# A decode step with cached attention and a gated MLP: two w_out blocks in one six-group transfer, their products dealt round the column groups, and fewer, wider copies

## The chip, the core and the metric

The kernel runs on one core of a Trainium2 chip. The metric is the device time of one execution in microseconds (us); three executions of the kernel before the change gave a median of 709.77 us (709.28 to 710.01). Every number is in fp32.

The engines are named as in the profile: PE multiplies matrices (PEld loads its stationary operand), DVE and POOL work on vectors, ACT does activations, SP issues transfers. The transfers themselves are moved by 16 DMA engines that all of the core's queues share.

## What is computed

One token for each of 8 batch rows, width 512. With `xn = layernorm(x)`:

```python
q = (xn @ wq).reshape(8, 32, 128)                 # wq: 512 x 4096
k, v = repeat(cache, 4)                           # 8 kv heads, 4096 positions, 128 wide
s = softmax(q . k * 128**-0.5) . v                # per batch row and head
s = s.reshape(8, 4096) @ wo                       # wo: 4096 x 512
z = gelu(xn @ w_in)                               # w_in: 512 x 1792
z1, z2 = z[:, :896], layernorm(z[:, 896:])
g = silu((z1 * (w_sp * z2 + b_sp)) @ w_out)       # w_out: 896 x 512
out = x + s * g
```

The keys are loaded in 16 pieces of 8.4 MB, the values in as many; with `wq`, `wo` and the MLP's weights about 291 MB are read.

## The kernel before, in words

All large operands pass through `ring`, a pool of three slots of 128 x 16384 fp32 (8.4 MB each). A slot can be loaded again when the last instruction that reads it is done. SP issues the loads in the order of the program text, and an issue that waits for its slot holds back all issues behind it. The order is: the MLP's weights (slot 1), `wq` (slot 2), keys of head 0, first half of the batch (slot 3, "k00"), keys of head 0, second half ("k01", slot 1 again), values "v00" (slot 2 again), "v01" (slot 3 again), keys of head 1 "k10", and so on for 8 heads, then `wo` in seven pieces.

PE also takes its work in the order of the text: `mlp()`, `project_q(0)`, `project_q(1)`, then for each head `scores` for two halves, `softmax`, `values` for eight batch rows, and last the product with `wo`. So slot 1 is free for k01 when the last product of `mlp()` that reads weights is done, slot 2 is free for v00 when `project_q(1)` is done, and slot 3 for v01 when the first `scores` is.

PE's array is used in four column groups of 32 columns (`R = 32`, `G = 4`): a product with at most 32 output rows is written to partitions 32g to 32g+31 of a PSUM bank, and products for different g can be issued one after another.

`mlp()` computes `xn @ w_in` (L144), gelu, the inner layernorm and the gate on DVE (L148 to L177), and then the product with `w_out`, here called the tail. The 896 rows of `w_out` are seven blocks of 128 rows. Blocks 0, 2, 4 and 6 (`MAIN`) lie on 128 partitions, behind `w_in` in the transfer `w_mlp` (L66). Blocks 1, 3 and 5 lie on few partitions: three transfers `w_low` (L72) of 8, 4 and 2 groups of `LOW_R = 4` rows bring them as 22 chunks of 32, 16 and 8 rows, side by side in the columns. For the tail, the gated activations `u` are transposed on PE (L179 for `MAIN`, L192 for the chunks), copied to SBUF by DVE (L180, L193) and multiplied: four `MAIN` products, one per column group (L184), and 22 chunk products (L196). A chunk of block j goes to column group `j // 2`, so that chunks that follow one another mostly share a group:

```python
for i, (j, r) in enumerate(some):
    g = j // 2
    nc.tensor.matmul(pw[R * g:R * (g + 1), :], hL[p0:p0 + n, i, R * g:R * (g + 1)],
                     w_low[:, lo + i, :], start=False, stop=((j, r) in LAST))
```

PSUM tiles named `scr` come from a pool of two banks used in turn; the tail's sum `pw` lies in `sc`, a fixed bank.

`project_q` writes the queries into `qz` by 32 copies of 128 x 4 for each quad of heads (L226), and `softmax` writes the transposed weights into `pT` by four copies of 128 x 128 per 512 columns (L270). `values` reads `pT` as `pT[:, j, b, :]` (L280).

Outside the tail, the change touches the tile of `xn` (L118), `hy` (L134, L135), `qz` (L86) and the host's packing of `w_out` (L366 to L385).

Of the kernel before, what the change touches and what calls it, by code (L numbers as in the profile page):

```python
# [8 lines left out]
F32 = mybir.dt.float32  # L9
# [4 lines left out]
P = 128  # L14
B, D = 8, 512
HKV, REP, S, DH = 8, 4, 4096, 128
NK = D // P
G = 4
J = S // (G * P)
R = 32  # L20
# [21 lines left out]


@with_exitstack
def tile_gqa_gmlp_decode(ctx: ExitStack, tc: tile.TileContext, x, side, kT, v, wq, wo,
                         w_mlp, lows, out):
# [22 lines left out]
    low_sb = []  # L69
# [10 lines left out]
    ident = const.tile([P, P], F32, name="ident")  # L80
# [20 lines left out]
    sc = ps_fix.tile([P, 2, 512], F32, name="sc")  # L101
# [29 lines left out]
    def mlp():  # L131
        zu = work.tile([P, 4, FQ], F32, name="zu", tag="p")
        z, u = zu[:, :2], zu[:, 2:]
        hy = work.tile([P, 2 * D], F32, name="hy", tag="pT")  # L134
        hT, hL = hy[:, :P], hy[:, P:].rearrange("p (a s) -> p a s", s=P)  # L135
        y_sb, e = zu[:, :2].rearrange("p a f -> p (a f)"), zu[:, 2, :P]
        pz = scratch([P, 2 * FQ], "pz")
        nc.vector.memset(pz, 0.0)
        for part in range(2):
            for k in range(NK):  # L140
                for g in range(G):
                    lo = g * FQ
                    n = min(FQ, FH - lo)
                    nc.tensor.matmul(pz[R * g:R * (g + 1), part * FQ:part * FQ + n], xnT[:, k, :],  # L144
                                     w_in_sb[:, k, part * FH + lo:part * FH + lo + n],
                                     start=(k == 0), stop=(k == NK - 1))
# [30 lines left out]
        nc.vector.tensor_mul(u[:, 1, :], z2, z1)  # L177
        th = scratch([P, P], "th")
        nc.tensor.transpose(th, u[:, 1, :P], ident)  # L179
        nc.vector.tensor_copy(hT, th)  # L180
        pw = sc[:, 0, :]
        for i, j in enumerate(MAIN):
            g = j // 2
            nc.tensor.matmul(pw[R * g:R * (g + 1), :], hT[:, R * g:R * (g + 1)], w_out_sb[:, i, :],  # L184
                             start=True, stop=(j == 6))
        for (ne, p0, _, chunks), w_low in zip(LOW, low_sb):
            n = ne * LOW_R
            for lo in range(0, len(chunks), 4):
                some = chunks[lo:lo + 4]
                tl = scratch([n, len(some) * P], "tl")  # L190
                for i, (j, r) in enumerate(some):
                    nc.tensor.transpose(tl[:, i * P:(i + 1) * P], u[:, 1, P + r:P + r + n], ident)  # L192
                nc.vector.tensor_copy(hL[p0:p0 + n, :len(some)].rearrange("p a s -> p (a s)"), tl)  # L193
                for i, (j, r) in enumerate(some):
                    g = j // 2
                    nc.tensor.matmul(pw[R * g:R * (g + 1), :], hL[p0:p0 + n, i, R * g:R * (g + 1)],  # L196
                                     w_low[:, lo + i, :], start=False, stop=((j, r) in LAST))
        nc.vector.tensor_copy(y_sb, pw)
# [10 lines left out]
    def project_q(quad):  # L209
        pq = scratch([P, REP * DH], "pq")  # L210
        for k in range(NK):
            for g in range(G):
                lo = (quad * G + g) * REP * DH
                nc.tensor.matmul(pq[R * g:R * (g + 1), :], xnT[:, k, :], wq_sb[:, k, lo:lo + REP * DH],  # L214
                                 start=(k == 0), stop=(k == NK - 1))
        q_sb = work.tile([P, REP * DH], F32, name="q_sb", tag="p")
        nc.vector.tensor_scalar(q_sb, pq, float(DH) ** -0.5, None, op0=ALU.mult)
        tq = scratch([P, REP * P], "tq")
        for r in range(REP):
            nc.tensor.transpose(tq[:, r * P:(r + 1) * P], q_sb[:, r * DH:(r + 1) * DH], ident)  # L220
        tv = tq.rearrange("p (r g c) -> p r g c", r=REP, g=G)
        for g in range(G):
            h = quad * G + g
            for b in range(B):
                o = b * R + b * REP
                nc.vector.tensor_copy(qz[:, h, o:o + REP], tv[:, :, g, b])  # L226

# [12 lines left out]
    def softmax(h):  # L240
# [22 lines left out]
        nc.vector.tensor_scalar(p, p, w, None, op0=ALU.mult)  # L263
        pT = work.tile([P, J, B, G * REP], F32, name="pT")
        for c in range(2):
            t = scratch([P, 512], "t")
            for j in range(4):
                nc.tensor.transpose(t[:, j * P:(j + 1) * P], p[:, 4 * c + j, :], ident)  # L268
            for j in range(4):
                nc.vector.tensor_copy(  # L270
                    pT[:, 4 * c + j].rearrange("p b (g r) -> p g b r", g=G),
                    t[:, j * P:(j + 1) * P].rearrange("p (g b r) -> p g b r", g=G, b=B))
        return pT

    def values(b, pT, v_unit):
        o = o_ps[b % 2]
        of = o.rearrange("p g d -> p (g d)")
        for j in range(J):
            c = j % G
            nc.tensor.matmul(of[R * c:R * c + G * REP, :], pT[:, j, b, :],  # L280
                             v_unit[:, j], start=(j < G), stop=(j >= J - G))
        o_all = small.tile([P, G, DH], F32, name="o_all")
        nc.vector.tensor_mul(o_all, o, diag[:, :, None].to_broadcast([P, G, DH]))  # L283
        o_sb = small.tile([P, DH], F32, name="o_sb")
        nc.vector.tensor_reduce(o_sb, o_all.rearrange("p g d -> p d g"), op=ALU.add, axis=AX.X)  # L285
        return o_sb
# [110 lines left out]
```

## Time and profile before

| what | value |
|---|---|
| median of three executions | 709.77 us (709.28 to 710.01) |
| the profiled execution, its own time | 710.74 us |
| its span, first to last instruction | 708.9 us |
| PE busy | 417.8 us, 59% of the span |
| DVE busy | 176.7 us, 25% |
| packets on the main DMA queue q1 | 6550, 290.79 MB |
| bytes over the span | 411 GB/s on average |

A row of the page's second part gives 40 slices of 17.7 us each; a digit is the busy share in tenths, and PEclk is the granted clock of PE in tenths of full speed. In a group of instructions, `x44` is the count, followed by the busy time in us, the mean duration of one in ns, and the idle time of the engine just before them with what ended it. One fp32 matmul of the program text stands as two records in the trace. In the chain of waits, each row is a start, a duration and what the time went to. In a table of stretches, DMA is the mean busy share of the 16 DMA engines; a packet counts in the stretch in which it starts, so short stretches can show more than 1.

### The profile page before, as it was taken

Reading aid. Unit: us, or ns where it says so; the run is one execution under the profiler, and the core shown is the slowest. Engines: PE = TensorE matmul, PEld = TensorE weight load, DVE = VectorE, ACT = ScalarE, POOL = GpSimd, SP = SyncE. Lnnn points to the kernel's source line nnn. Section 1 sums busy time; section 2 is a strip of 40 time slices with the busy share of each in tenths; the row PEclk is TensorE's granted clock in tenths of the full one; section 3 lists DMA queues with packets and bytes.
Section 4 is the critical chain, followed back from the end, with each engine's and each line's share of the span. In section 5 each row is a group of like instructions: output and inputs, shape, how many; then the busy total and the mean of one; then the engine's idle time right before and its main releaser. Section 6 shows DMA issues by size and latency. Waiting matters only on the chain.

```text
span 708.9 us, 5936 instructions
## 1 busy us (share of the span) xinstructions
PE 417.8 (59%) x2667; PEld 124.1 (18%) x2667; DVE 176.7 (25%) x376; ACT 13.5 (2%) x27; POOL 3.7 (1%) x11
## 2 busy tenths in 40 slices
PE   2499875545665556554556557554554475655676
PEld 1221222111211112111211112110111121111222
DVE  2400312340144004230234014210234024400450
ACT  0000000000000000000000000000000000000000
POOL 1000000000000000000000000000000000000000
PEclk9655696777677767776777677787777667776797
DMA  9990599999999999999999999999999999999996
GB/s 386 447 404 26 237 415 463 418 423 459 415 429 453 411 436 451 411 440 445 414 441 437 425 433 441 429 430 437 433 426 437 441 422 430 444 423 429 412 427 255
DMA packets 6735, 291.25 MB, mean 411 GB/s; under 512 B 758, under 2 KB 1014, under 8 KB 1406
## 3 DMA queue, kind: packets, MB, share of 16 engines
q1 hardware_dynamic: 6550, 290.79, 95.2%
q8 instruction: 21, 0.34, 0.2%
q10 hardware_dynamic: 160, 0.08, 0.0%
q14 instruction: 4, 0.03, 0.0%
HBM read 290.80 MB, written 0.07 MB: 410 GB/s over the span
## 4 chain that ended last, share of the span: by engine, by line
DMA 72%; PE 22%; issue 4%; DVE 1%; SPq 0%; POOLq 0%; POOL 0%
DMA slot<-in_kT 34%; DMA slot<-in_v 32%; PE sc L237 7%; PE o_ps L280 6%; DMA slot<-in_wo 6%; PE sc L196 5%; PE scr L214 1%; PE sc L340 1%; PE scr L192 1%; PE po_ps L289 0%; DVE o_sb L285 0%; PE sc L184 0%; DMA x_sb<-in_x 0%; DVE o_all L283 0%; SPq L317 0%
## 5 line engine op out<-in xcount | busy, mean ns | idle before, releaser
L237 PE MATMUL sc<-slot,qz 128*32 128x512 f32 x1024 | 148.8, 746 | 122.6 <-DMA slot<-in_kT 122.6
L280 PE MATMUL o_ps<-slot,pT 128*16 128x512 f32 x1024 | 151.8, 733 | 73.9 <-DMA slot<-in_v 73.9
L283 DVE TENSOR_TENSOR o_all<-o_ps,diag 128x512 f32<-128x512 f32 x64 | 44.2, 691 | 148.9 <-PE o_ps L280 148.8
L242 DVE TENSOR_REDUCE nm<-sc 128x1 f32<-128x1024 f32 x8 | 9.8, 1224 | 268.0 <-PE sc L237 268.0
L237 PEld LDWEIGHTS sc<-slot,qz 128*32 128x32 f32 x1024 | 36.1, 133 | 228.8 <-DMA slot<-in_kT 130.5
L285 DVE TENSOR_REDUCE o_sb<-o_all 128x128 f32<-128x512 f32 x64 | 67.8, 1060 | 2.2
L280 PEld LDWEIGHTS o_ps<-slot,pT 128*16 128x16 f32 x1024 | 29.6, 111 | 153.9 <-issue 103.6
L289 PE MATMUL po_ps<-fold,o_sb 128*128 128x4 f32 x128 | 24.7, 263 | 28.4 <-DVE o_sb L285 28.4
L196 PE MATMUL sc<-slot,hy 16*32 16x512 f32 (+2 forms) x44 | 38.8, 1056 | 0.8 <-DVE hy L193 0.8
L289 PEld LDWEIGHTS po_ps<-fold,o_sb 128*128 128x128 f32 x128 | 19.0, 188 | 73.5 <-DVE o_sb L285 72.3
L268 PE MATMUL scr<-ident,p 128*128 128x128 f32 x64 | 15.0, 412 | 10.7 <-DVE p L263 10.7
L244 ACT ACTIVATE p<-sc,nm 128x1024 f32<-128x1024 f32 x8 | 8.9, 1113 | 566.1 <-DVE nm L242 566.1
L270 DVE COPY pT<-scr 128x128 f32<-128x128 f32 x64 | 13.9, 283 | 9.6 <-PE scr L268 9.6
L268 PEld LDWEIGHTS scr<-ident,p 128*128 128x128 f32 x64 | 12.0, 214 | 11.1 <-issue 11.1
L193 DVE COPY hy<-scr 16x512 f32<-16x512 f32 (+3 forms) x6 | 3.8, 635 | 34.9 <-PE sc L196 25.4
L144 PE MATMUL scr<-slot,xnT 128*32 128x256 f32 (+1 forms) x64 | 6.5, 549 | 9.3 <-DMA slot<-in_w_mlp 9.3
L196 PEld LDWEIGHTS sc<-slot,hy 16*32 16x32 f32 (+2 forms) x44 | 6.6, 163 | 27.7 <-issue 23.9
L247 PE MATMUL scr<-ident,nm 128*1 128x128 f32 x8 | 2.2, 270 | 10.9 <-DVE nm L242 10.9
L214 PE MATMUL scr<-slot,xnT 128*32 128x512 f32 x64 | 8.4, 672 | 0.0
L260 PE MATMUL scr<-wl,same 128*128 128x1 f32 x16 | 3.8, 309 | 6.2 <-DVE wl L258 6.2
L331 PE MATMUL sc<-slot,oT 128*8 128x512 f32 x32 | 6.0, 878 | 1.3 <-DMA slot<-in_wo 1.3
L340 PE MATMUL sc<-slot,oT 128*8 128x128 f32 x128 | 5.3, 334 | 1.4 <-DMA slot<-in_wo 1.4
(86 smaller groups left out, 81.9 us busy)
## 6 DMA issues: line engine op xcount, KB each, us to landing
slot<-in_v SPq DMA_DIRECT2D x4, 2048.0 KB, 39.5
slot<-in_wo SPq DMA_DIRECT2D x3, 2048.0 KB, 34.1
slot<-in_w_mlp SPq DMA_DIRECT2D x1, 4608.0 KB, 13.8
slot<-in_wo SPq DMA_DIRECT2D x1, 1024.0 KB
slot<-in_wo SPq DMA_DIRECT2D x1, 512.0 KB, 33.3
slot<-in_wo SPq DMA_DIRECT2D x2, 256.0 KB, 28.9
slot<-in_w_low SPq DMA_DIRECT2D x1, 384.0 KB
slot<-in_w_low SPq DMA_DIRECT2D x1, 256.0 KB
```

Of the source, the lines that this page charges most:

```text
L196: nc.tensor.matmul(pw[R * g:R * (g + 1), :], hL[p0:p0 + n, i, R * g:R * (g + 1)], w_low[:, lo + i, :], start=False, stop=((j, r) in LAST))
L214: nc.tensor.matmul(pq[R * g:R * (g + 1), :], xnT[:, k, :], wq_sb[:, k, lo:lo + REP * DH], start=(k == 0), stop=(k == NK - 1))
L237: nc.tensor.matmul(sc[R * g:R * (g + 1), c, :], qz[:, h, b * R:(b + 1) * R], k_sb[:, i, c, g, :], start=(b == 0), stop=(b == B - 1))
L242: nc.vector.tensor_reduce(m, sc, op=ALU.max, axis=AX.XY, negate=True)
L244: nc.scalar.activation(p.rearrange("p j s -> p (j s)"), sc.rearrange("p c s -> p (c s)"), AF.Exp, bias=m, accum_out=l[:, h:h + 1])
L268: nc.tensor.transpose(t[:, j * P:(j + 1) * P], p[:, 4 * c + j, :], ident)
L270: nc.vector.tensor_copy(pT[:, 4 * c + j].rearrange("p b (g r) -> p g b r", g=G), t[:, j * P:(j + 1) * P].rearrange("p (g b r) -> p g b r", ...
L280: nc.tensor.matmul(of[R * c:R * c + G * REP, :], pT[:, j, b, :], v_unit[:, j], start=(j < G), stop=(j >= J - G))
L283: nc.vector.tensor_mul(o_all, o, diag[:, :, None].to_broadcast([P, G, DH]))
L285: nc.vector.tensor_reduce(o_sb, o_all.rearrange("p g d -> p d g"), op=ALU.add, axis=AX.X)
L289: nc.tensor.matmul(po[:, b * REP:(b + 1) * REP], o_sb, fold, start=True, stop=True)
L340: nc.tensor.matmul(acc[R * g:R * g + B, :], oT[:, h, r, :], wo_sb[:, m, g * P:(g + 1) * P], start=(m == FOLDED), stop=(m == HKV * REP - 1))
```

## The change

Five blocks of `w_out` (0, 2, 4, 6 and now 5) come with `w_mlp` on 128 partitions. The other two (1 and 3) come by one transfer of 6 groups of 4 rows: 24 partitions that each hold, for each block, 6 chunks of 512 columns (five chunks of 24 rows and one of 8; `CH = 6`). The 17 products of the tail (5 and 12) are issued round the four column groups, whatever their block, into a bank of the pool of two instead of `sc`. For them, 2 transposes and one copy prepare the five large products, and 6 transposes and 6 copies the chunks. `xn` moves into unused columns of slot 1, behind the MLP's weights. `qz` rows are 288 instead of 256 long, so that one copy of 128 x 32 per head can write all eight batch rows; `pT` is laid out by batch row first and written by one copy of 128 x 512 per 512 columns.

```diff
-MAIN = [0, 2, 4, 6]
-LOW_R = 4
-def rows_of(j, lo, hi, n):
-    return [(j, r) for r in range(lo, hi, n)]
-LOW = [(8, 0, 0, rows_of(1, 0, P, 32) + rows_of(5, P // 2, P, 32)),
-       (4, 0, 6 * D, rows_of(3, 0, P, 16)), (2, R, 6 * D, rows_of(5, 0, P // 2, 8))]
-LAST = [(1, 96), (3, 112), (5, 56)]
+LOW_E, LOW_R = 6, 4
+QR = LOW_E * LOW_R
+CH = -(-P // QR)
+MAIN = [0, 2, 4, 6, 5]
+LOW = [1, 3]
+N_LOW = len(LOW) * CH * D
...
+    n_low = n_mlp + N_LOW
     nc.sync.dma_start(mlp_slot[:, :n_mlp], w_mlp)
+    nc.sync.dma_start(mlp_slot[:QR, n_mlp:n_low],
+                      w_low[:, :LOW_R * N_LOW].rearrange("e (i n) -> e i n", n=N_LOW))
-    for (e, p0, c0, chunks), w_low in zip(LOW, lows):
-        t = mlp_slot[p0:p0 + e * LOW_R, n_mlp + c0:n_mlp + c0 + len(chunks) * D]
-        nc.sync.dma_start(t, w_low[:, :LOW_R * len(chunks) * D].rearrange("e (i n) -> e i n", i=LOW_R))
-        low_sb.append(t.rearrange("p (c d) -> p c d", d=D))
+    w_low_sb = mlp_slot[:QR, n_mlp:n_low].rearrange("p (j a d) -> p j a d", a=CH, d=D)
...
-    qz = const.tile([P, HKV, B * R], F32, name="qz")
+    qz = const.tile([P, HKV, B * (R + REP)], F32, name="qz")
...
-    xn = work.tile([B, D], F32, name="xn", tag="pT")
+    xn = from_slot(B, D)
...
-        th = scratch([P, P], "th")
-        nc.tensor.transpose(th, u[:, 1, :P], ident)
-        nc.vector.tensor_copy(hT, th)
-        pw = sc[:, 0, :]
...
+        th = scratch([P, 2 * P], "th")
+        for a in range(2):
+            nc.tensor.transpose(th[:, a * P:(a + 1) * P], u[:, 1, a * P:(a + 1) * P], ident)
+        nc.vector.tensor_copy(hT.rearrange("p a s -> p (a s)"), th)
+        for lo in range(0, CH, 4):
+            n = min(4, CH - lo)
+            tl = scratch([QR, n * P], "tl")
+            for a in range(lo, lo + n):
+                k = min(QR, P - a * QR)
+                nc.tensor.transpose(tl[:k, (a - lo) * P:(a - lo + 1) * P],
+                                    u[:, 1, P + a * QR:P + a * QR + k], ident)
+            for a in range(lo, lo + n):
+                k = min(QR, P - a * QR)
+                nc.vector.tensor_copy(hL[:k, a], tl[:k, (a - lo) * P:(a - lo + 1) * P])
+        pw = scratch([P, D], "pw")
+        todo = [(hT[:, j % 2, R * (j // 2):R * (j // 2 + 1)], w_out_sb[:, i, :]) for i, j in enumerate(MAIN)]
+        for a in range(CH):
+            k = min(QR, P - a * QR)
+            todo += [(hL[:k, a, R * (j // 2):R * (j // 2 + 1)], w_low_sb[:k, i, a, :])
+                     for i, j in enumerate(LOW)]
+        for i, (lhsT, rhs) in enumerate(todo):
+            g = i % G
+            nc.tensor.matmul(pw[R * g:R * (g + 1), :], lhsT, rhs, start=(i < G), stop=(i + G >= len(todo)))
         nc.vector.tensor_copy(y_sb, pw)
...
-            for b in range(B):
-                o = b * R + b * REP
-                nc.vector.tensor_copy(qz[:, h, o:o + REP], tv[:, :, g, b])
+            nc.vector.tensor_copy(qz[:, h].rearrange("p (b s) -> p b s", b=B)[:, :, :REP],
+                                  tv[:, :, g, :B].rearrange("p r b -> p b r"))
...
-        pT = work.tile([P, J, B, G * REP], F32, name="pT")
+        pT = work.tile([P, B, J, G * REP], F32, name="pT")
...
-            for j in range(4):
-                nc.vector.tensor_copy(
-                    pT[:, 4 * c + j].rearrange("p b (g r) -> p g b r", g=G),
-                    t[:, j * P:(j + 1) * P].rearrange("p (g b r) -> p g b r", g=G, b=B))
+            nc.vector.tensor_copy(
+                pT[:, :, 4 * c:4 * c + 4].rearrange("p b j (g r) -> p (j g) b r", g=G),
+                t.rearrange("p (m b r) -> p m b r", b=B, r=REP))
...
-            nc.tensor.matmul(of[R * c:R * c + G * REP, :], pT[:, j, b, :],
+            nc.tensor.matmul(of[R * c:R * c + G * REP, :], pT[:, b, j, :],
                              v_unit[:, j], start=(j < G), stop=(j >= J - G))
```

The source of the low transfer on the host is a tensor of 6 rows, each of 4 x 6144 values with 64 values of padding behind.

More of the change, by code (lines that the diff above doesn't have):

```diff
@@ L30 @@
 FOLDED = 16
-MAIN = [0, 2, 4, 6]
-LOW_R = 4
-def rows_of(j, lo, hi, n):
-    return [(j, r) for r in range(lo, hi, n)]
-LOW = [(8, 0, 0, rows_of(1, 0, P, 32) + rows_of(5, P // 2, P, 32)),
-       (4, 0, 6 * D, rows_of(3, 0, P, 16)), (2, R, 6 * D, rows_of(5, 0, P // 2, 8))]
-LAST = [(1, 96), (3, 112), (5, 56)]
+LOW_E, LOW_R = 6, 4
[4 more added lines that the diff above has]
+N_LOW = len(LOW) * CH * D
 @with_exitstack
 def tile_gqa_gmlp_decode(ctx: ExitStack, tc: tile.TileContext, x, side, kT, v, wq, wo,
-                         w_mlp, lows, out):
+                         w_mlp, w_low, out):
     nc = tc.nc
@@ L134, in mlp @@
         hy = work.tile([P, 2 * D], F32, name="hy", tag="pT")
-        hT, hL = hy[:, :P], hy[:, P:].rearrange("p (a s) -> p a s", s=P)
+        hT = hy[:, :2 * P].rearrange("p (a s) -> p a s", a=2)
+        hL = hy[:QR, 2 * P:2 * P + CH * P].rearrange("p (a s) -> p a s", a=CH)
         y_sb, e = zu[:, :2].rearrange("p a f -> p (a f)"), zu[:, 2, :P]
@@ L177, in mlp @@
         nc.vector.tensor_mul(u[:, 1, :], z2, z1)
-        th = scratch([P, P], "th")
-        nc.tensor.transpose(th, u[:, 1, :P], ident)
-        nc.vector.tensor_copy(hT, th)
-        pw = sc[:, 0, :]
[L182 to L197, printed above, removed]
+        th = scratch([P, 2 * P], "th")
@@ L368 @@
     w2 = c(B_w_out).reshape(NB, P, D)
-    lows = {}
-    for i, (e, _, _, chunks) in enumerate(LOW):
-        n = e * LOW_R
-        t = np.stack([w2[j, r:r + n] for j, r in chunks])
-        t = t.reshape(len(chunks), e, LOW_R, D).transpose(1, 2, 0, 3).reshape(e, -1)
-        lows[f"w_low{i}"] = np.concatenate([t, np.zeros((e, 64), np.float32)], axis=1)
+    low = np.zeros((len(LOW), CH * QR, D), np.float32)
+    low[:, :P] = w2[LOW]
+    low = low.reshape(len(LOW), CH, LOW_E, LOW_R, D).transpose(2, 3, 0, 1, 4).reshape(LOW_E, -1)
+    low = np.concatenate([low, np.zeros((LOW_E, 64), np.float32)], axis=1)
     arrays = {
@@ L384 @@
             w2[MAIN].transpose(1, 0, 2).reshape(P, len(MAIN) * D)], axis=1),
-        **lows,
+        "w_low": low,
     }
@@ L391 @@
     with tile.TileContext(nc) as tc:
-        n = len(args) - len(LOW)
-        tile_gqa_gmlp_decode(tc, *args[:n], args[n:], out)
+        tile_gqa_gmlp_decode(tc, *args, out)
     r = run(nc, [{f"in_{name}": a for name, a in arrays.items()}], core_ids=[0])
```

6 lines of the change are left out of this document (5 added, 1 removed).

## The prediction

> **What bounds the kernel now.** I read the page's slices first, then the chain of waits, then what SP's queue waited for, then single stretches.
>
> ```profile
> DMA  9990599999999999999999999999999999999996
> ...
> q1 hardware_dynamic: 6550, 290.79, 95.2%
> q8 instruction: 21, 0.34, 0.2%
> ...
> DMA 72%; PE 22%; issue 4%; DVE 1%; SPq 0%; POOLq 0%; POOL 0%
> ```
>
> The transfers run at nine tenths or more everywhere but in the fourth and fifth slices (53 to 89 us) and at the end. So the kernel is bound by its bytes, with one hole. While q1's packets run, one DMA engine moves 290.79 MB / (16 x 0.952 x 708.9 us) = 26.93 GB/s, all of them 431. The hole, from the chain of waits, SP's waits and the tables of stretches:
>
> ```profile
> 71.25 7.04 PE sc L196 x8
> ...
> 85.76 3.62 PE scr L214 x32
> 89.37 0.02 issue
> 89.39 31.44 DMA slot<-in_v
> ```
> ```profile
> SPq L293 <- PE sc L196: 57.5, 1, 57.5
> SPq L293 <- DMA slot<-in_w_low: 16.3, 3, 11.9
> ```
> ```profile
> 44.00:84.00 40.00, 38.44 (x88) 7.72 (x86) 5.17 (x9) 0.31 (x1) 0.00 (x0) 0.53 0.37 154
> 84.00:700.00 616.00, 353.50 (x2348) 104.42 (x2344) 158.61 (x331) 11.26 (x24) 0.00 (x0) 0.74 1.00 432
> ```
>
> SP stood 57.5 us in front of k01's issue (L293) until the last chunk product of the tail (L196) ended at 78.29. Between 44 and 84 us the engines were busy 0.37 of the time: 0.63 x 40 = 25.2 us of mean idle time. From 84 to 700 us the share is 1.00. Only this hole can be won; what it is worth depends on which of the 16 engines ends last. Its ends:
>
> ```profile
> 3.91 74.73 SPq L293 DMA_DIRECT2D slot<-in_kT  x2
> ```
> ```profile
> DMA to landing us min/median/max: 55.5/55.5/55.5
> ```
> ```profile
> 50.00:51.00 1.00, 1.00 (x2) 0.17 (x1) 0.00 (x0) 0.00 (x0) 0.00 (x0) 0.50 0.91 393
> 51.00:52.00 1.00, 1.00 (x3) 0.27 (x2) 0.00 (x0) 0.00 (x0) 0.00 (x0) 0.50 0.76 328
> 52.00:53.00 1.00, 1.00 (x3) 0.25 (x2) 0.00 (x0) 0.00 (x0) 0.00 (x0) 0.50 0.31 131
> 78.00:79.00 1.00, 0.28 (x1) 0.00 (x0) 0.68 (x1) 0.00 (x0) 0.00 (x0) 0.50 0.00 0
> 79.00:80.00 1.00, 0.94 (x12) 0.60 (x16) 0.22 (x2) 0.00 (x0) 0.00 (x0) 0.50 2.69 918
> ```
>
> The first row is SP's for k00 and k01, the second k00's landing (L293 up to 60 us): issued at 3.91, landed on its last engine 55.5 later, at 59.4. The share falls below one after 50; a packet of 64 KB takes 65.5 / 26.93 = 2.43 us and counts where it starts, so the earliest engines ran dry at about 52.5. k01's packets start at about 79.3, 1.0 us after PE let go. So the earliest engines idled 26.8 us, the last 19.9.
>
> **The change part by part.** *Transfers.* `w_mlp` grows by 128 x 512 x 4 = 262 KB; the low part shrinks from 786 KB to 24 x 24.6 = 590 KB. Together 66 KB more, 0.15 us. `w_mlp` lands 262 / 431 = 0.61 us later, and with it L144 and the chain behind it:
>
> ```profile
> 14.67 6.46 PE L144 MATMUL scr<-slot,xnT 128*32 128x256 f32 x64 [9.32 <-DMA slot<-in_w_mlp]
> 31.17 0.43 DVE L177 TENSOR_TENSOR zu<-zu 128x256 f32<-128x256 f32 x1
> 31.65 0.47 PE L179 MATMUL scr<-ident,zu 128*128 128x128 f32 x1 [2.38 <-DVE zu L177]
> 31.92 1.06 PE L192 MATMUL scr<-ident,zu 128*32 128x128 f32 x4
> 32.16 0.29 DVE L180 COPY hy<-scr 128x128 f32<-128x128 f32 x1 [0.57 <-PE scr L179]
> 32.91 1.94 PE L184 MATMUL sc<-slot,hy 128*32 128x512 f32 x8
> 34.78 7.03 PE L196 MATMUL sc<-slot,hy 32*32 32x512 f32 x8
> 42.38 0.41 DVE L193 COPY hy<-scr 32x256 f32<-32x256 f32 x1 [8.69 <-PE scr L192]
> ```
>
> *The tail before*, from L177's end to 78.29: 46.7 us, of which the 44 records of L196 are most. They run one behind the other: 7.03 us for 8, 0.85 from one start to the next. L184's 8 records, four products in four column groups, need 1.94 us in all: they run beside one another.
>
> *The tail after* starts at 31.6 + 0.6 = 32.2. Two transposes take 0.5 + 0.2 (a further one of L192's four), the first four chunks' about as long as L192's 1.06: 34.0. The copy of the large pair (0.41) lies beside them. `pw` takes the bank of the first chunks, so the products wait for four copies of 24 x 128, by L180's 0.29 and 0.03 between: 35.3. The other two transposes and copies lie beside the first products. 17 products over four groups are five rounds, by L184 1.94 each: 9.7 us. End at 45.0 instead of 78.29.
>
> *The ring later on*, which the change leaves as it is, from the chain of waits:
>
> ```profile
> 131.55 47.35 DMA slot<-in_kT
> ...
> 597.08 49.19 DMA slot<-in_kT
> 646.27 0.04 issue
> 646.32 9.86 PE sc L237 x64
> ```
>
> From 178.90 (131.55 + 47.35) to 646.27 are 24 slots: 19.5 us each, 8.39 MB at 431 GB/s. An issue that lands 49.2 us later has 29.7 us of earlier traffic (49.19 - 19.47) ahead of it, so compute has that much slack per slot.
>
> *What is late next.* k01's issue then stands ready at 45.0, its packets could start at 46.0, and the earliest engine is dry at 52.5 + 0.6 = 53.1. The hole closes with 7 us to spare; that part of the tail's 33 us buys nothing. v00 waits for `project_q`: 78.29 to 89.37 before, 11.1 us, so 56.1 after; it is needed when k01 has gone by, at 53.1 + 19.5 = 72.6. v01 waits for the first `scores`, with k00 landed at about 57 and the longest run of 64 products in the chain 9.9 us, so 67; needed at 92. Behind k01's issue on SP stand exactly these, in this order, and none is late.
>
> *Which engine ends last.* For the earliest engine four terms count. It idled 26.8 us. `w_mlp` takes 0.61 of them. k01's first packets were slow, which a waiting queue spares: 918 KB, 14 packets, start between 79 and 80, and 2.69 x 16 / 14 is 3.07 us each, 0.64 over 2.43. And PE's instructions come by the same engines, 21 packets (q8) of 16 KB, 0.60 us each; one of them came ahead of the hole and was made good in it:
>
> ```profile
> q8 instruction: 1, 0.02, 0.3%
> ```
>
> (the queues between 40 and 60 us). Now it stays on some engine. 26.8 - 0.61 + 0.64 - 0.60 = 26.2 us won. The six groups carry 4 x 24.6 = 98 KB each, 3.65 us; if the engines that have them are also those that fall behind later, 3.65 of the 26.2 are lost: 22.5. If the engine that ends last is spared `w_mlp`'s part and the instructions, the most is 27.4. I take 26.2, the end nearest to the mean row's 25.2 - 0.15 = 25.0: the groups' 3.65 us need not add up with delays that 21 packets spread over other engines.
>
> A rule of the Trainium skill bears on how the groups fall: "DMA: Bandwidth & Descriptors", section "Why a DMA increments its semaphore by 16 and not by 1", says that such a transfer uses the largest number of engines up to 16 that divides the outer sizes of both sides, which for 6 and 24 is six. No row here numbers the engines; by that rule one engine would not get it all, which is a rival below.
>
> *Copies.* L226's and L270's work lies beside transfers:
>
> ```profile
> L270 DVE COPY pT<-scr 128x128 f32<-128x128 f32 x64 | 13.9, 283 | 9.6 <-PE scr L268 9.6
> L226 DVE COPY qz<-scr 128x4 f32<-128x4 f32 x64 | 4.6, 150 | 1.5 <-PE scr L220 1.5
> L325 DVE COPY oT<-po_ps 128x32 f32<-128x32 f32 x8 | 1.5, 191 | 3.8 <-PE po_ps L289 3.8
> L198 DVE COPY zu<-sc 128x512 f32<-128x512 f32 x1 | 0.7, 691 | 7.1 <-PE sc L196 7.1
> ```
>
> 64 small `qz` copies (4.6 us) become 8 of about 0.19 (L325): 3.1 us less of DVE, twice half of it after a `project_q`, inside v00's and v01's slack. Four `pT` copies (1.13) become one of 0.69 (L198): 0.9 us less per head ahead of `values`, which then wait for the landing of v. Worth nothing, and in the 29.7 us if it goes the other way. `xn` in slot 1 would cost something if it had to wait for the slot's transfers; L144 read the slot at 14.67 while SP still waited for `w_low` (16.3 us from about 4, so until 20), so columns, not slots, are waited for. Even then the tail would end at about 51, still in time. `qz`'s wider clearing makes one POOL instruction an eighth longer, in the 9.32 us in which L144 waits for its data.
>
> *Sum*: 710.74 - 26.2 = 684.5 for an execution like the profiled one, whose span would be 682.7. The median of the runs shown is 0.97 lower: 709.77 - 26.2 = **683.6 us**.
>
> **Rivals.** *The products do not overlap.* All chunks use the same rows of the array, and L196 never shows two groups in turn. Then 34 records at 0.85 and the start at 35.3 give 64.5; k01 starts 78.3 - 64.5 = 13.8 us earlier: 696.0. A rule of the Trainium skill says so: "TensorE: Matmul & The Clock Gate", "Part 3: Packing small matmuls", has a weight load overlap a running product only when the row group differs. L184 speaks against it, four products with the same rows in 1.94 us, so I hold it unlikely.
>
> *The low transfer goes by one engine.* 590 KB at 26.93 GB/s are 21.9 us; k00 lands there at 53.1 + 21.9 = 75.0, and every later slot waits for that engine: 26.2 - 21.9 = 4.3 us won, 705.5. Against it: SP waited for `w_low` only until 20, and k00's engines ended between 52.5 and 59.4, so the old transfers with 8, 4 and 2 groups were shared.
>
> *Slower: the wide `pT` copy.* It writes 128 runs of four elements with larger strides. If a run cost what L226's 4-element copy does, 150 ns, a copy would take 19.2 us and `softmax` 36 us more per head. From 29.7 us per head on the ring runs dry: 6.4 us for each of 8 heads, 51 us, 683.6 + 51 = 735. Against it: L270's copies have 32 such runs already and take 0.283.
>
> *It doesn't do what it says*: something else, not the tail, frees slot 1. Then 709.8. Against it stands SP's row, a single wait of 57.5 us for L196.
>
> **How the numbers follow.** Forecast 0.85; no overlap 0.07; one engine 0.03; slower copy 0.03; no effect 0.02. The measurement tells 0.2%, 1.4 us, from no change. Faster: 0.85 + 0.07 + 0.03 = 0.95; same 0.02; slower 0.03. The range takes the forecast's two ends, 709.77 - 22.5 = 687.3 and 709.77 - 27.4 = 682.4, with half a us for repeats: 681.9 to 687.8. The rivals lie outside it and hold 0.15.
>
> **What would show it.** Right: the slices of DMA without a hole; SP's long wait for the tail's last product down from 57.5 to about 24 us; 34 records of products in about 10 us; k00's last engine done at 57 and k01's at 76; the last `wo` landing about 26 us earlier; landings still 19.5 apart. Wrong: the products' records 0.85 apart in a line (no overlap); a landing of k00 at 75 (one engine); a `pT` copy of several us; DMA below 9 in any slice after the third; or landings more than 19.6 apart, with an engine that carries both a low group and the later delays.

## The result, and the profile after

The kernel after the change takes 685.42 us (median of four executions, 685.31 to 687.15). The kernel before, run beside it, takes 709.52 us (median of four, 709.27 to 710.01). The ratio is 0.9665, with a 95% interval of 0.9648 to 0.9682: 24.1 us less, where 26.2 were forecast. The profiled execution took 685.31 us and has a span of 683.5; before it was 710.74 and 708.9, so the two spans differ by 25.4.

The first view is the page: its DMA slices, the queues and the chain's shares by engine.

```profile
DMA  9999999999999999999999999999999999999995
...
q1 hardware_dynamic: 6510, 290.85, 98.7%
q8 instruction: 20, 0.33, 0.2%
...
DMA 80%; PE 15%; issue 4%; DVE 1%; SPq 0%; POOLq 0%; POOL 0%
```

The hole in the fourth and fifth slices is gone. The bytes are the same within 0.06 MB, the share of q1 rises from 95.2% to 98.7%, and DMA's part of the chain from 72% to 80%. The queue of SP says the same, as its waits for the tail and for the low transfer show:

```profile
SPq L295 <- PE scr L201: 22.3, 1, 22.3
...
SPq L295 <- DMA slot<-in_w_low: 3.5, 1, 3.5
```

SP now stands 22.3 us in front of k01's issue where it stood 57.5. The chain of waits at that place:

```profile
34.87 6.27 PE scr L201 x34
41.15 36.29 DMA slot<-in_kT
```

The tail ends at 41.14 instead of 78.29, and k01 lands 36.3 us after its issue, behind k00. In the table of stretches, the third row is the one that showed 0.37 before; the first two are the tail's products:

```profile
34.80:38.20 3.40, 3.33 (x10) 0.56 (x10) 0.41 (x3) 0.00 (x0) 0.00 (x0) 0.51 0.85 366
38.20:41.20 3.00, 2.90 (x25) 0.66 (x24) 0.04 (x1) 0.00 (x0) 0.00 (x0) 1.00 1.18 508
44.00:84.00 40.00, 23.60 (x172) 6.67 (x168) 3.15 (x12) 0.00 (x0) 0.00 (x0) 0.77 1.00 430
84.00:675.00 591.00, 326.35 (x2208) 97.20 (x2196) 150.01 (x217) 11.27 (x24) 0.00 (x0) 0.75 1.00 431
```

The engines are busy from 44 us to the end at 1.00. No other wait for PE leaves them idle. So the time came from the place that the prediction named; what is left to explain is why 24 to 25 us came and not 26.2, and which part of the change did it.

For both questions the ends of the single DMA engines are needed. Each transfer is counted off by 16 engines; the table has the first and the last of the 16 for k00, for k01 and for the last piece of `wo`, in us from the start of the span, of all the kernels that follow. It is worked out from the landings in each trace.

```
kernel          tail ends  k00 landed     k01 landed      last wo piece    last-first  span   median us
before            78.29    52.61..59.43   99.48..101.33   700.37..705.11      4.7      708.9   709.52
after             41.14    53.26..58.08   72.61..77.44    673.22..679.99      6.8      683.5   685.42
e1_one_group      51.1     53.15..59.08   73.43..78.43    674.06..682.07      8.0      685.6   685.95
e2_two_groups     41.6     53.16..58.73   72.62..78.09    673.12..681.70      8.6      685.2   685.82
e3_old_copies     40.3     53.10..58.19   72.46..77.55    672.98..680.28      7.3      683.8   685.96
e4_low_twice      39.3     53.14..61.68   72.49..81.03    673.25..683.53     10.3      687.2   689.33
e5_before_round   49.0     52.63..59.46   71.99..78.81    672.52..680.43      7.9      684.4   686.03
e6_all_main       38.3     54.53..56.32   73.88..75.67    674.42..679.41      5.0      683.0   684.80
e7_one_low4       40.3     53.75..57.30   73.10..76.65    674.01..678.68      4.7      682.2   684.19
e8_low_first      53.4     53.23..57.73   75.37..77.58    675.93..680.66      4.7      684.2   686.68
e9_one_column     62.3     53.29..58.79   83.63..85.53    684.21..689.14      4.9      692.9   695.04
```

The first engine ends 700.37 - 673.22 = 27.15 us earlier than before, the last 705.11 - 679.99 = 25.1. The profiled executions of e1 and e2 took 688.14 and 687.65 us, 2.2 and 1.8 above their medians, so the last landings in their rows are those of longer executions.

### The profile page after: what moved, and what is told of

Same layout as the page of the kernel before. It is cut to its first block, busy times and chain, and to the rows that moved or that the text cites. A ratio compares the mean times of both kernels' runs of the same rounds, so it can differ in the third digit from the quotient of the medians.

```text
span 683.5 us, 5757 instructions
## 1 busy us (share of the span) xinstructions
PE 373.0 (55%) x2634; PEld 115.1 (17%) x2634; DVE 168.0 (25%) x272; ACT 13.5 (2%) x27; POOL 3.9 (1%) x11
## 3 DMA queue, kind: packets, MB, share of 16 engines
q1 hardware_dynamic: 6510, 290.85, 98.7%
## 4 chain that ended last, share of the span: by engine, by line
DMA 80%; PE 15%; issue 4%; DVE 1%; SPq 0%; POOLq 0%; POOL 0%
DMA slot<-in_kT 41%; DMA slot<-in_v 35%; PE sc L240 8%; PE o_ps L282 5%; DMA slot<-in_wo 4%; PE scr L201 1%; PE po_ps L291 0%; DMA x_sb<-in_x 0%; DVE o_sb L287 0%; PE scr L188 0%; SPq L302 0%; DVE hy L192 0%; DVE o_all L285 0%; DVE st L119 0%; PE scr L181 0%
## 5 line engine op out<-in xcount | busy, mean ns | idle before, releaser
L240 PE MATMUL sc<-slot,qz 128*32 128x512 f32 x1024 | 144.1, 726 | 136.1 <-DMA slot<-in_kT 136.1
L271 PE MATMUL scr<-ident,p 128*128 128x128 f32 x64 | 14.8, 410 | 10.7 <-DVE p L266 10.7
L272 DVE COPY pT<-scr 128x512 f32<-128x512 f32 x16 | 11.1, 692 | 10.8 <-PE scr L271 10.8
L145 PE MATMUL scr<-slot,xnT 128*32 128x256 f32 (+1 forms) x64 | 6.4, 547 | 9.6 <-DMA slot<-in_w_mlp 9.6
L201 PE MATMUL scr<-slot,hy 24*32 24x512 f32 (+2 forms) x34 | 6.2, 726 | 0.5 <-DVE hy L192 0.5
L266 DVE TENSOR_SCALAR p<-p,w 128x1024 f32<-128x1024 f32 x8 | 6.0, 753 | 0.3
L145 PEld LDWEIGHTS scr<-slot,xnT 128*32 128x32 f32 x64 | 3.4, 161 | 12.2 <-issue 12.1
```

What stands on the lines that cost most here:

```text
L201: nc.tensor.matmul(pw[R * g:R * (g + 1), :], lhsT, rhs, start=(i < G), stop=(i + G >= len(todo)))
L240: nc.tensor.matmul(sc[R * g:R * (g + 1), c, :], qz[:, h, b * R:(b + 1) * R], k_sb[:, i, c, g, :], start=(b == 0), stop=(b == B - 1))
L272: nc.vector.tensor_copy(pT[:, :, 4 * c:4 * c + 4].rearrange("p b j (g r) -> p (j g) b r", g=G), t.rearrange("p (m b r) -> p m b r", b=B, r ...
```

## The experiments

My theory after the result had two parts. *The tail:* the products dealt round the column groups run beside one another, so k01's issue is ready before the engines run dry, and everything beyond that is worth nothing. *The engines:* the last engine ends later against the first one (6.8 us, before 4.7) because one of the six that carry a low group also carries instruction packets. The rivals: the order round the groups does not matter, since the repacking alone shortens the tail enough; or the copies brought a part of it; or the last engine's lag has nothing to do with the low groups.

**e1: the products in order of column group.** The packing stays, the round goes.

```diff
+        groups = [i * G // len(todo) for i in range(len(todo))]
...
-            g = i % G
-            nc.tensor.matmul(pw[R * g:R * (g + 1), :], lhsT, rhs, start=(i < G), stop=(i + G >= len(todo)))
+            g = groups[i]
+            nc.tensor.matmul(pw[R * g:R * (g + 1), :], lhsT, rhs, start=(g not in groups[:i]),
+                             stop=(g not in groups[i + 1:]))
```

> The changed kernel with its 17 tail products issued one column group after the other (5, 4, 4, 4) instead of round the groups; all else as in the changed kernel (685.42). Theory A (the gain is the hole in the transfers, closed because products of different column groups run beside one another): the 34 records stand 0.85 us apart again, so the tail ends at 34.9 + 29.0 = 63.9 instead of 41.1, later than the 52.3 that the transfers allow; a hole opens again, and the time is that of the kernel before less the difference of the tail's ends, 709.5 - (78.3 - 63.9) = 695.1. Rival B (it is the repacking, 17 products and 8 transposes for 26 and 23, that brings the gain; or products do not overlap in any order): 685.4. A hole of about 11 us in the DMA slices decides too.

Measured: 685.95 us, ratio 0.9654 [0.9633, 0.9675], the same as the changed kernel's. The miss is in the tail's duration. The timeline and the table of stretches of e1:

```profile
35.11 16.00 PE L202 MATMUL scr<-slot,hy 128*32 128x512 f32 x34 [0.54 <-DVE hy L192]
```
```profile
35.00:38.50 3.50, 3.39 (x4) 0.71 (x5) 0.45 (x3) 0.00 (x0) 0.00 (x0) 0.50 1.04 449
38.50:45.70 7.20, 7.20 (x23) 1.79 (x23) 0.00 (x0) 0.00 (x0) 0.00 (x0) 0.97 0.98 421
45.70:51.20 5.50, 5.41 (x10) 0.90 (x6) 0.06 (x1) 0.00 (x0) 0.00 (x0) 0.50 1.05 453
```

The records stand in a line 0.85 us apart at first, but PE's clock (last column but two) goes to full at 38.5, and the spacing halves until about 45.7. Nor do all of them stand in a line: from 42.95 on two or three weights are loaded at once in some of these steps, which e8 comes back to.

```profile
42.52 0.10 PEld L202 LDWEIGHTS scr<-slot,hy 24*32 24x32 f32 x1 [0.33 <-issue]
42.95 0.14 PEld L202 LDWEIGHTS scr<-slot,hy 24*32 24x32 f32 x3 [0.32 <-issue]
```

The tail ends at 51.1. By the prediction's numbers that is inside the limit of 53.1 - 1.0 = 52.1, but the landings put the limit earlier: k01's first one comes 73.43 - 53.15 = 20.28 us after k00's, where the changed kernel has 72.61 - 53.26 = 19.35, so the first engines still idled 0.9 us. In a kernel with this packing, then, the round is not what closes the hole, but for that last part: the first part of my theory fell as I had put it.

**e2: two column groups in turn**, first the lower pair, then the upper one.

```diff
+        half = (len(todo) + 1) // 2
+        groups = [2 * (i // half) + i % half % 2 for i in range(len(todo))]
```

> As the changed kernel, but the tail's products alternate between two column groups at a time: 9 rounds instead of 5. Theory A: 9 rounds of at most 1.71 us end at 50.3, still ahead of the 52.3 until which k01's issue costs nothing: 685.4, within 0.5. Rival C (every us of the tail counts, as it does on the path from the tail to project_q and scores): up to 9 us longer, about 694.

Measured: 685.82 us, 0.9659 [0.9638, 0.9681]. The timeline of e2:

```profile
33.98 7.61 PE L203 MATMUL scr<-slot,hy 128*32 128x512 f32 x34 [0.54 <-DVE hy L192]
```

7.61 us of records instead of 6.22, and no difference in the time. But the tail ends at 41.6 and not at the 50.3 that was expected, half a us after the changed kernel's, so this run hardly tests what the tail's length costs; e5, with 49.0, does.

**e3: the old copies.** `qz`, `pT` and `xn` as before the change, the MLP as after it.

```diff
-        pT = work.tile([P, B, J, G * REP], F32, name="pT")
+        pT = work.tile([P, J, B, G * REP], F32, name="pT")
...
-            nc.vector.tensor_copy(qz[:, h].rearrange("p (b s) -> p b s", b=B)[:, :, :REP],
-                                  tv[:, :, g, :B].rearrange("p r b -> p b r"))
+            for b in range(B):
+                o = b * R + b * REP
+                nc.vector.tensor_copy(qz[:, h, o:o + REP], tv[:, :, g, b])
```

> The changed kernel with the three side edits undone: 64 small qz copies, four pT copies per 512 columns in the old layout, xn in its own tile. Theory A: these lie beside transfers, 685.4 within 0.5. Rival D (the copies on the way from scores to values count): 0.9 us per head and 3.1 us of qz copies, up to 10 us longer, 692 to 696.

Measured: 685.96 us, 0.9657 [0.9638, 0.9675]. The groups of the changed kernel, then those of e3:

```profile
L272 DVE COPY pT<-scr 128x512 f32<-128x512 f32 x16 | 11.1, 692 | 10.8 <-PE scr L271 10.8
...
L228 DVE COPY qz<-scr 128x32 f32<-128x32 f32 x8 | 1.0, 183 | 1.5 <-PE scr L224 1.5
```
```profile
L274 DVE COPY pT<-scr 128x128 f32<-128x128 f32 x64 | 13.9, 284 | 9.9 <-PE scr L272 9.9
...
L230 DVE COPY qz<-scr 128x4 f32<-128x4 f32 x64 | 4.6, 152 | 1.5 <-PE scr L224 1.5
```

The new copies save 2.8 + 3.6 us of DVE and nothing of the time. The durations are as forecast (four times 284 ns become one of 692), but the 64 narrow `pT` copies partly overlap (13.9 us for 64 x 284 ns = 18.2), so their replacement saves 2.8 us over eight heads and not the 0.9 per head that the prediction had.

**e4: the low transfer twice.** The second load puts the same rows on 24 other partitions, where nothing reads them.

```diff
                       w_low[:, :LOW_R * N_LOW].rearrange("e (i n) -> e i n", n=N_LOW))
+    nc.sync.dma_start(mlp_slot[R:R + QR, n_mlp:n_low],
+                      w_low[:, :LOW_R * N_LOW].rearrange("e (i n) -> e i n", n=N_LOW))
```

> The changed kernel with the transfer of the six groups issued a second time into rows 32 to 55 of the same columns, which nothing reads. It adds 590 KB. Theory E (each of six DMA engines carries one group, the slowest of the 16 engines ends the kernel, and it is one of these six): 98 KB more on each, 3.65 us longer, 689.1. Rival F (the mean over the engines counts): 590 KB at 431 GB/s, 1.4 us longer, 686.8. If the engines with groups were not among the last, the 2.3 us by which the last engine's landing lies behind the next ones would have to be passed first: 685.4 to 687. One engine for all of it: 21.9 us longer.

Measured: 689.33 us, 0.9705 [0.9688, 0.9723]: 3.9 us slower than the changed kernel, while 590 KB spread over all engines would be 590 / 431 = 1.4. The lags of the 16 engines behind the first of them, for k00 in the changed kernel, for k00 in e4, and for the last piece of `wo` in both:

```
after, k00   0.0 0.0 0.0 0.1 0.3 0.3 0.3 0.5 0.8 1.7 3.6 3.6 3.7 4.0 4.3 4.8
e4, k00      0.0 0.0 0.1 0.2 0.2 0.4 0.4 0.5 1.0 2.1 7.3 7.4 7.4 7.5 7.9 8.5
after, wo    0.0 0.2 0.2 3.0 3.2 3.5 3.5 3.6 3.8 4.1 4.5 4.6 4.6 4.7 5.7 6.8
e4, wo       0.0 0.2 0.3 2.9 2.9 3.3 3.8 4.4 4.6 4.9 7.1 7.3 7.7 7.8 9.3 10.3
```

Exactly six engines lag by 3.6 to 4.8, and by 7.3 to 8.5 when the transfer is doubled: the 3.65 us of a group of 98 KB. That agrees with the rule of the Trainium skill, "DMA: Bandwidth & Descriptors", section "Why a DMA increments its semaphore by 16 and not by 1". At the end of the span the first engine is where it was (673.25) and the last is 683.53 - 679.99 = 3.5 later. The chain shows that the last one is what counts:

```profile
33.61 5.66 PE scr L203 x34
...
658.95 24.59 DMA slot<-in_wo
```

The tail is over earlier than in the changed kernel, and the last landing, 658.95 + 24.59 = 683.5, is later.

**e5: the round without the packing.** The kernel before, with its 22 chunk products dealt round the four column groups. Chunks with `p0` above 0 are summed in the second half of `sc`, and one DVE addition joins both.

```diff
...
-                    g = j // 2
-                    nc.tensor.matmul(pw[R * g:R * (g + 1), :], hL[p0:p0 + n, i, R * g:R * (g + 1)],
-                                     w_low[:, lo + i, :], start=False, stop=((j, r) in LAST))
+                    g, s = done % G, j // 2
+                    done += 1
+                    to = sc[:, 1, :] if p0 else pw
+                    nc.tensor.matmul(to[R * g:R * (g + 1), :], hL[p0:p0 + n, i, R * s:R * (s + 1)],
+                                     w_low[:, lo + i, :], start=(14 < done <= 18),
+                                     stop=(10 < done <= 14 or done > 18))
...
+        nc.vector.tensor_add(y_sb, y_sb, sc[:, 1, :])
```

> The kernel before with its 22 chunk products issued round the four column groups; the eight of the third transfer go to a second bank, added by one more DVE instruction; transfers and copies as before. Theory A (the hole is all; the round of groups alone can close it too): each of the six batches takes about 1.0 us of transposes, 0.2 of the rest of the copy and 1.9 of products, so the tail ends near 52.5, the hole is at most 2 us, and the first engine ends 26 us earlier. The engines of the third transfer carry 177 KB, 6.7 us, and end last: 686.5 to 690.5. Rival B (the repacking is needed): products shrink only a little, 700 or more.

Measured: 686.03 us, 0.9657 [0.9641, 0.9673], 0.5 below the expected range, with a tail that ends earlier than expected. The table of stretches of e5:

```profile
33.70:41.40 7.70, 7.70 (x34) 1.63 (x30) 1.09 (x2) 0.00 (x0) 0.00 (x0) 0.50 0.97 419
41.40:49.00 7.60, 6.82 (x36) 1.28 (x32) 2.04 (x3) 0.00 (x0) 0.00 (x0) 0.50 0.95 414
44.00:84.00 40.00, 27.52 (x200) 7.55 (x192) 9.79 (x73) 0.31 (x1) 0.00 (x0) 0.73 1.01 438
```

The tail ends at 49.0, at half the clock throughout, and that is enough: the DMA share from 44 to 84 us is 1.01, and k01's first landing is 71.99 - 52.63 = 19.36 us after k00's, so no hole is left. With e1's 0.9 us at 51.1, the limit for the tail's end lies between 49.0 and 51.1. e1 and e5 together: the packing without the round closes the hole but for 0.9 us, and the round without the packing closes it. The tail of 46.7 us had to lose 27 to 29 of them.

**e6: no low transfer.** All seven blocks lie on 128 partitions, behind `w_in`.

```diff
-MAIN = [0, 2, 4, 6, 5]
-LOW = [1, 3]
+MAIN = [0, 2, 4, 6, 5, 1, 3]
```

(and `w_low`, its transposes, its copies and its products go).

> The changed kernel with all seven blocks of w_out on 128 partitions in w_mlp and no transfer of groups: 7 products, 2 transposes, 1 copy in the tail. Theory E (the engine that ends last is one with a group, 3.65 us, and two of PE's instruction packets, about 1.5 us each; without groups the last are those with three such packets): every engine carries 33 KB more, 1.2 us; the last landing falls from 6.8 us behind the first engine's to 4.7: 1.2 - 2.1 = 0.9 us faster, 684.5. Rival F (the mean over the engines counts, and bytes fall by 66 KB): 685.3. Rival I (a later landing of w_mlp, 1.2 us, is on the path): 686.6.

Measured: 684.80 us, 0.9643 [0.9629, 0.9658]. The timeline of e6:

```profile
34.67 3.64 PE L177 MATMUL scr<-slot,hy 128*32 128x512 f32 x14 [0.52 <-DVE hy L172]
```

14 records in four groups, 3.64 us. The first engine ends 1.2 us later than in the changed kernel (674.42 against 673.22), since each of the 16 carries an equal part of the two blocks; the last one ends 0.6 earlier, since the lag is 5.0 and not 6.8. The time alone, 684.80, lies between the 684.5 of the theory and the 685.3 of the rival F; it is the landings that speak for the theory.

**e7: one low block, in four groups.** Six blocks on 128 partitions, block 1 as 4 groups of 4 rows.

```diff
-LOW_E, LOW_R = 6, 4
-MAIN = [0, 2, 4, 6, 5]
-LOW = [1, 3]
+LOW_E, LOW_R = 4, 4
+MAIN = [0, 2, 4, 6, 5, 3]
+LOW = [1]
...
-        hL = hy[:QR, 2 * P:2 * P + CH * P].rearrange("p (a s) -> p a s", a=CH)
+        hL = from_slot(QR, CH * P).rearrange("p (a s) -> p a s", a=CH)
```

> The changed kernel with six blocks in w_mlp and one by a transfer of 4 groups (8 chunks of 16 rows, 64 KB per group). Theory E: all engines carry 16 KB more, 0.6 us, four of them 2.4 us. If none of the four gets PE's instruction packets, the last landing is that of an engine with three packets, 4.7 us behind the first: 1.5 us faster than the changed kernel, 683.9. If one of them does, 2.4 + 3.1 = 5.5 behind: 0.7 us faster, 684.7. Rival F: 685.4.

Measured: 684.19 us (684.12 to 684.21), 0.9634 [0.9619, 0.9648], the fastest version of this study. The intervals of e7 and of the changed kernel just meet at 0.9648, but each of e7's executions is below each of the changed kernel's. The chain of e7:

```profile
35.10 5.20 PE scr L201 x28
...
654.06 24.62 DMA slot<-in_wo
```

The last landing is at 678.68, 1.3 us before the changed kernel's, at a lag of 4.7, that of the kernel before. So the low groups do cost what the engines' theory says, and 1.2 us is the most that either of the two other divisions of the rows brought.

**e8: one column group after the other, the low chunks first.** After e1 the clock was the suspect: that tail was short because five 128-row products ran first. Here they run last.

```diff
+        todo = todo[len(MAIN):] + todo[:len(MAIN)]
+        groups = [i * G // len(todo) for i in range(len(todo))]
```

(with the product's lines as in e1).

> As e1_one_group (one column group after the other), but the 12 chunk products before the 5 products of 128 rows. In e1 PE's granted clock rose to full 3.4 us after the 128-row products began, so the 34 records took 16.0 us, ended at 51.1, and no hole opened (685.95): the round of groups is not needed where the clock rises. Theory G (products on at most 24 rows in one column group do not raise the clock, as 44 records in a line did not in the kernel before; those on 128 rows do): 24 records at 0.85 from 35.1 end at 55.6, the 128-row ones at about 62; the hole is back, 16.3 us shorter than before, 709.5 - 16.3 = 693.2. Rival H (any unbroken line of products raises the clock; what kept it low before were the pauses for transposes and copies): end at about 51, 686.

Measured: 686.68 us, 0.9668 [0.9653, 0.9682], a miss by 6.5 us. The table of stretches and PE's weight loads in e8:

```profile
34.60:48.40 13.80, 13.78 (x24) 2.62 (x24) 0.36 (x2) 0.00 (x0) 0.00 (x0) 0.50 1.03 443
48.40:51.00 2.60, 2.60 (x7) 0.56 (x7) 0.00 (x0) 0.00 (x0) 0.00 (x0) 0.50 0.93 403
51.00:53.40 2.40, 2.35 (x6) 0.49 (x4) 0.01 (x1) 0.00 (x0) 0.00 (x0) 0.98 0.51 218
44.00:84.00 40.00, 31.48 (x204) 8.24 (x204) 4.81 (x15) 0.31 (x1) 0.00 (x0) 0.83 0.97 412
```
```profile
38.88 0.17 PEld L203 LDWEIGHTS scr<-slot,hy 24*32 24x32 f32 x1 [0.68 <-issue]
39.74 0.18 PEld L203 LDWEIGHTS scr<-slot,hy 24*32 24x32 f32 x3 [0.68 <-issue]
...
48.41 0.19 PEld L203 LDWEIGHTS scr<-slot,hy 128*32 128x32 f32 x4 [1.66 <-issue]
```

The clock behaved as expected: 0.50 for all 13.8 us of the chunks, and full 2.7 us after the first 128-row product. But 24 records took 13.8 us, not 24 x 0.85 = 20.4: from 39.74 on, several weights are loaded at once in many of the 0.85 us, around the places where the order of the program passes from one column group to the next. The time is nearer to the rival's 686, but its reason, a clock that any unbroken line of products raises, is not what the rows show. The tail ended at 53.4, and the first engines idled 2.8 us (75.37 - 53.23 = 22.14, against 19.35). The hole was small, and the last engine ends only 680.66 - 679.99 = 0.7 later than in the changed kernel although the first ends 2.7 later: in a hole the engines that lag catch up (a lag of 2.2 at k01 instead of 4.8, and of 4.7 at the end instead of 6.8).

**e9: all products in one column group**, so that no pair can form; a DVE clearing of `pw` serves the three unused groups.

```diff
+        todo = todo[len(MAIN):] + todo[:len(MAIN)]
+        groups = [0] * len(todo)
+        nc.vector.memset(pw, 0.0)
```

(with the product's lines as in e1).

> As e8_low_first, but all 17 products of the tail into column group 0; the other three are cleared by one DVE instruction first. In e8 records of two groups ran in pairs at the changes of group, so the tail ended at 53.4 and the hole was short. Theory A with E: here nothing runs in pairs; 24 records at 0.85 and 10 of 128 rows, the last six at 0.43, end near 61.3, and the first engine's packets come about 9.7 us later than in the changed kernel. The hole lets the engines with groups catch up, so the last landing is 4.7 us behind the first as in the kernel before, not 6.8: 9.7 - 2.1 = 7.6 us longer than the changed kernel, 693.0. Rival J (the hole counts in full): 695.1. Rival B (the order of groups does not matter at all, only the number of products): 686.

Measured: 695.04 us, 0.9791 [0.9775, 0.9808]. The slices, SP's wait and the table of stretches of e9:

```profile
DMA  9995999999999999999999999999999999999996
```
```profile
SPq L299 <- PE scr L204: 43.6, 1, 43.6
```
```profile
34.90:55.00 20.10, 20.10 (x24) 3.96 (x24) 0.00 (x0) 0.00 (x0) 0.00 (x0) 0.50 0.91 392
55.00:60.00 5.00, 5.00 (x7) 1.07 (x7) 0.00 (x0) 0.00 (x0) 0.00 (x0) 0.50 0.03 13
60.00:62.30 2.30, 2.29 (x5) 0.33 (x3) 0.00 (x0) 0.00 (x0) 0.00 (x0) 0.96 0.00 0
44.00:84.00 40.00, 34.03 (x168) 8.37 (x166) 4.80 (x15) 0.31 (x1) 0.00 (x0) 0.80 0.78 332
```

Now the line in one column group does what e1 was meant to do: with the changed kernel's packing and its transfers, the tail ends at 62.3, the hole opens again in the fourth slice, and 9.6 us of the gain are gone. That the column groups never matter is thereby excluded. What is left of the gain, 709.80 - 695.04 = 14.8 us against the kernel before beside it, the packing brings with no products side by side. The time alone, 695.04, is that of the rival, 695.1, and not 693.0. The landings decide: the first engine ends 684.21 - 673.22 = 11.0 us later, the last 689.14 - 679.99 = 9.15. The rival has both later by the same 9.7. So the engines did catch up, by 1.8 us, and what the expected number had too small is the hole, 11.0 for the first engine and not 9.7; 1.0 of that is the tail's end, 62.3 instead of 61.3.

## Why the prediction was right, and in which step its gain was too high

*What bounds the kernel:* right. SP's wait for the last product of the tail made the hole, and closing it is the whole gain. e3 leaves the side edits nothing, and e9 brings the hole back by the products' column group and order, with transfers and copies as after the change and one DVE clearing more.

*The tail:* the mechanism was right, its end too late: 41.1 instead of 45.0. It began as forecast: in the timeline the gate's last instruction ends at 32.3 (forecast 32.2) and the products start at 34.9 (35.3).

```profile
15.43 6.42 PE L145 MATMUL scr<-slot,xnT 128*32 128x256 f32 x64 [9.62 <-DMA slot<-in_w_mlp]
...
34.87 6.22 PE L201 MATMUL scr<-slot,hy 128*32 128x512 f32 x34 [0.54 <-DVE hy L192]
```

L145 starts 0.76 later than L144 did (forecast 0.61). The five rounds take 6.2 us and not 9.7, since the clock rose 3.3 us after they began (38.15); through the whole of the old tail, 34.78 to 78.29, it had stood at 0.50. By the forecast's own argument the 4 us are worth nothing, and e1, e2 and e5 with tails to 51.1, 41.6 and 49.0 take the same time within 0.6 us. The forecast's limit of 52.1 was 1 to 3 us too late, as e5 and e1 show, but 8 us were to spare even so.

*The rival of no overlap* is excluded: 34 records in 6.22 us. The rule that the prediction cited beside it, "TensorE: Matmul & The Clock Gate", "Part 3: Packing small matmuls" in the Trainium skill, does not hold for these products, which share their rows and differ in the column group; e9, where they share the column group too, has them 0.85 us apart. The table of the same page, "Measured speedup vs the span model", gives three column groups 2.38 times one; that agrees better with the rows of before, where 8 records take 1.94 us round four groups (L184) and 7.03 in one (L196), 3.6 times. *The low transfer by one engine* is excluded by the six lags of e4, *the slow wide copy* by its 692 ns (forecast 0.69 us), *no effect* by the result.

*What comes next:* v00 was forecast to be issued at 56.1 and v01 at 67. In SP's timeline v00 is issued at 52.37, and the issue of v01 is done 15.18 later, at 67.55:

```profile
52.37 15.18 SPq L302 DMA_DIRECT2D slot<-in_v  x2
```

Both in time, and v00 earlier by what the tail gained.

*Which engine ends last:* here is the step that was mis-sized. For the first engine the terms hold: 26.8 - 0.61 + 0.64 = 26.8 forecast without an instruction packet, 27.15 measured. For what the last engine loses against it, the prediction took off one instruction packet at 0.60 and let the six groups' 3.65 us cost nothing, as they "need not add up with delays that 21 packets spread over other engines". The 0.60 was too small by the prediction's own row of q8 between 40 and 60 us: 0.3% of 16 engines' 20 us is 0.96. And the two do add up in part: the lag of the last engine grew from 4.7 to 6.8, 2.0 us where 0.60 stood. The steps of the lags tell how, though the trace numbers no engine: of the six lags that the groups left, 3.8 becomes 5.3 between the landings at 227 and 247 us, and 6.8 between those at 498 and 518, and a packet of PE's instructions starts in each of the two stretches, at 238 and at 515. So the engine that ends last has a group and meets two packets, which hold it up by about 1.5 each. In the kernel before, the lag of 4.7 grows from 1.85 at k01 by the same steps, to 3.1 and 4.7, as that of engines with packets only; its old low groups had left 6.8 at k00, and the hole let all engines run dry and start anew. So the hole had been wiping out what the low groups cost, and the change that removes the hole brings that cost back. e4 shows it by its reverse (+3.5 us on the last engine for 3.65 more in the groups), e7 by its removal (lag 4.7). 27.15 - 2.0 = 25.1 us on the last landing, 25.4 in the span. The medians differ by 24.1, since the profiled execution of before lies 1.2 us above its median and that of after 0.1 below: of the 2.1 us between 26.2 and 24.1, 0.8 belong to this step and 1.3 to the executions that were profiled.

The prediction had named this step among its signs of being wrong: an engine that carries both a low group and the later delays, with landings more than 19.6 apart. That engine is there; but the last landings of k00 and of the first keys of head 7, 58.08 and 601.96, are 28 slots apart, 19.4 us each. Which of the sixteen engines get the instruction packets is not shown, as the trace doesn't number them.

## What to carry to other kernels

In a kernel bound by its transfers, a chain that holds back an issue costs the time from when the first engine runs dry until the issue, and not the chain's length: work out that limit first, since any of several shortenings that get under it brings the same. Then look at which engine ends last, not at their mean: rows packed on few partitions load a few engines, and what these lag behind is kept to the end unless a hole lets them catch up.

## What the runs showed of the hardware

- *PE's clock depends on the rows that the products use, not only on PE being busy.* 24-row products of 32 columns left it at 0.50 with PE busy without a gap: 13.8 us in e8, 20.1 in e9. 128-row ones of 32 columns, behind them in the same two kernels, were followed by the full clock 2.7 us (e8) and 4.7 us (e9) after the first of them; in e1 it was 3.4 us, in the changed kernel 3.3. The number of cells in use does not explain it by itself: four products of 32 rows and 32 columns side by side use as many as one of 128 rows, and the rounds of e5, of 32 rows and fewer, did not raise it in 15 us. Nor is it shown that a round of 24-row products keeps it up: in the changed kernel it was full from 38.15 to 41.56, in e1 from 38.54 to 45.37, and fell 3.2 and 4.2 us after the first 24-row product. In the clock records of these traces each change lies a multiple of 3.41 us after the one before, so such delays tell the next step and not a time that PE needs.
- *Records of different column groups run beside one another even when the program issues one group after the other* (e8: 24 records in 13.8 us, with pairs around the changes of group, against 20.1 in one group in e9). The trace does not name the column group of a record, so how PE picks the pairs stays open.
- *A packet of PE's instructions costs its engine more than its bytes.* The 20 packets of 16 KB last about 1.06 us each where 0.60 were worked out from the rate of the large packets, and the engine's landings shift by 1.5.
